# The third block's second group of columns by 20 products instead of 22, and an earlier place for the weight sums

## The chip, the cores and the metric

The kernel runs on one core of a Trainium2 chip. The time is that of one execution on the device in microseconds (us); less is better. Three runs of the kernel before gave a median of 463.58 us. The core has TensorE (matmuls, into the eight banks of PSUM), VectorE and ScalarE (both read PSUM and write on-chip memory), GpSimd, and SyncE, whose queue issues the transfers. In the profile they are PE (PEld for the loading of weights), DVE, ACT, POOL and SP.

## What is computed

A gated recurrence over a sequence, for 4 x 8 heads of 48 channels and 768 steps, is followed by a feed-forward part on 3072 tokens. All is fp32.

```python
for t in range(S):
    state = f[:, :, t, :, None] * state + np.einsum('bhd,bhe->bhde', k[:, :, t], v[:, :, t])
    y[:, :, t] = np.einsum('bhd,bhde->bhe', q[:, :, t], state)
x = np.ascontiguousarray(y.transpose(0, 2, 1, 3)).reshape(B * S, H * D)   # 3072 x 384
a = x @ w1            # 384 x 1024
b = x @ w2            # 384 x 1024
h = a * b @ w3        # 1024 x 1024
return h @ w_out      # 1024 x 384
```

`w3 @ w_out` is folded into one matrix of 1024 x 384 in the kernel, so each token block goes up (`a`, `b`, their product) and down (one matrix).

## The kernel before

The sequence is cut into 24 chunks of 128 steps (u = 0 to 23), and the tokens into six blocks of 512 (n = 0 to 5), each of four chunks. A chunk passes through `front` (loads, gates, forward and backward scans on VectorE, factors Q and K, L526 to L556), a visit of TensorE (L579, L653, L672, L686), state sums on VectorE (L759, L762, L818) and a way through DRAM that turns its result into columns of the block's xt (L866, L869). The 24th chunk is over at about 256 us; from then on there is only feed-forward work.

The up part of a block has three forms:

- `part` (block 0): plain products.
- `seven(jc)` (blocks 1 and 2, four calls each): a Strassen-like scheme for two column tiles and two token halves, over three tiles of the inner dimension. It has the parts m1, m2, m6, m5, m7, m4 and m3, which hold 1, 2, 1, 1, 2, 2 and 2, so 11 products; each product is made for w1 and for w2, two matmuls of 128x128 by 128x256 (L993). ScalarE copies partial results (L1034, L1037), and VectorE adds (L1043) and multiplies a by b (L1040, L1046). Its token sums (`sums`) and weight sums (`w12t`, made early) lie in the tile `place`.
- `many(g)` (blocks 3 to 5, two calls each): a scheme of 20 products for four column tiles, two token halves and three inner tiles, where two `seven` take 22. Its products (L1148) stand in six chains (`CHAINS`); a chain owns a bank, and after a product that is used by itself ScalarE copies the bank (L1169) before the next product of the chain is added to it. In CHAINS, (a, b) is token operand a with weight operand b. Operands a from 6 are the 12 token sums X (`X_SUMS`, L1115, one set for a block); operands b from 12 are the 22 weight sums (`W_SUMS`, L1109, one set for the kernel). VectorE adds the products up by the 12 `Y_SUMS` (L1192) and multiplies a by b (L1204, and L1211 after a half copy L1208).

The down part is two calls of `down` in a block, each with seven products of four matmuls of 128x192 (L897, which `part` uses too), sums of its operands S0 to S3 (L1262) and of its results (L1275, L1288, L1299, L1305, L1313), two copies (L1269, L1282), and stores (L1318).

The weight sums have no buffers of their own. They are written over tiles of the attention (`homes`): floor, the two gates, the three q, two k, two f, then fwd, bwd, K, K and Q. The temporaries of `many` lie in a pool "t" of nine: the first four are those of `seven` (`aside` frees them when the last `seven` are done), the others lie in Q and ys tiles. Block 2's token sums X lie where `w12t` does.

Before the end the kernel checks the range of its inputs: ScalarE looks at all weights again in 34 pieces (L1536, L1540), which SP loads (L1532) into three buffers; VectorE joins the counts (L1548 to L1569), the verdict goes to DRAM and back as one row (L1574, L1578), and L1583 and L1584 reduce it. A branch on it closes the program.

The order of instructions is made by a planner when the program is built (`Plan`): each piece of work is added with an engine, a cost, dependencies, a priority (the lowest goes first among those that can start), and what it takes and frees in slots and pools (banks are the pool "f"). `listed` then plays the engines in time and emits the pieces in that order, so a change of one piece's cost or priority can move all that follow, on every queue. [...]

The weight sums have the priority `100 * MANY + W_LATE + k`, and depend on `over`: the last chunk's visit, sums and transfers. `SPREAD` is what the planner allows for a transfer of the verdict to land.

Of the kernel before, what the change touches and what calls it, by code (L numbers as in the profile page):

```python
# [66 lines left out]
KH = KF // 2  # L67
# [23 lines left out]
GAP = 0.2  # L91
FILL_FROM = 262.0
RELOAD = 6.0
SPREAD = 10.0
QLATE = 0.1
MANY = 3
W_LATE = 30
W_SINCE = 0.0
W_STEP = 0.0
CHAINS = [  # L100
# [193 lines left out]
def ranged(ctx, tc, q, k, f_logit, v, w1, w2, w3, w_out, out, ident, w12, wc, left):  # L294
# [71 lines left out]
    plan = Plan()  # L366
# [85 lines left out]
    tk = [{} for _ in range(NU)]  # L452
# [268 lines left out]
    def turning(u):  # L721

        s, t = st[u], tk[u]

        def turned():
            s["kt"] = work.tile([P, HP, R], F32, name="kt")
            nc.scalar.copy(s["kt"].rearrange("p (b two) r -> p b (two r)", two=2), s["pk"])

        if u < NPE:
            t["t"] = plan.add("PE", 0.45, lambda: turn(u), [t["k"]] + past(u, 1, "d"), need(u) - 999)  # L730
        else:
            t["t"] = plan.add("PE", 0.45, lambda: turn(u), [t["k"]], need(u) - 999, takes=["f"])
        t["e"] = plan.add(
            "ACT", 0.55, turned, [t["t"]] + past(u, 2, "s"), need(u), frees=[t["t"]] if u >= NPE else [],
        )

    def begin(u):

        def emit():
            pairs(u)  # L740
            update(u)

        t = tk[u]
        t["a"] = t["s"] = plan.add(
            "PE", 1.1, emit, [t["q"], t["k"], t["e"], t["lv"]] + past(u, 1, "m", "d"), need(u) - 999, slack=0.8,
        )
        paired(u)
# [142 lines left out]
    blk = [{} for _ in range(NB)]  # L890
    stores, upq, downq, w_nodes, opened = [], [], [], [], []
    over = plan.add("none", 0.0, lambda: None)

    def three(out_, lhs, rhs, start=True):

        for i in range(len(lhs)):
            nc.tensor.matmul(  # L897
                out_, lhsT=lhs[i], rhs=rhs[i], start=start and i == 0, stop=i == len(lhs) - 1,
                skip_group_check=True,
            )  # L900

    def ffn(n):
# [16 lines left out]
        def part(c0, c1, jcs):  # L919
            cols = slice(c0 * C, c1 * C)  # L920
            nt = (c1 - c0) * C
            cost = 6 * max(0.135, nt * 0.322 / 384)

            def up(jc, which):
                def emit():
                    s["pu", jc, which, c0] = bank()
                    three(
                        s["pu", jc, which, c0][:, 0:nt], [up_weights(w12, which, kc, jc) for kc in range(KM)],
                        [s["xt"][:, kc, cols] for kc in range(KM)],
                    )  # L930
                return emit

            def keep_a(jc):
                return lambda: nc.scalar.copy(a_b(jc)[:, cols], s["pu", jc, 0, c0][:, 0:nt])

            def times(jc):
                def emit():
                    ab = a_b(jc)[:, cols]
                    nc.vector.tensor_tensor(ab, s["pu", jc, 1, c0][:, 0:nt], ab, ALU.mult)
                return emit  # L940

            for jc in jcs:
                h = jc // KH
                x = [tk[n * UB + c]["x"] for c in range(c0, c1)]
                n0 = 100 * n + 50 + 10 * (jc >= KH)
                pa = plan.add("PE", cost, up(jc, 0), x + pieces[0, h], n0, takes=["f"])
                ka = takes_ab(jc, plan.add("ACT", 0.2 + nt * 0.28 / 384, keep_a(jc), [pa], -10, frees=[pa]))
                pb = plan.add("PE", cost, up(jc, 1), x + pieces[1, h] + [pa], n0 - 5, takes=["f"])
                kb = plan.add("DVE", 0.16 + nt * 0.4 / 384, times(jc), [pb, ka], -10, frees=[pb])
                s["up"] += [pa, pb]  # L950
                s["done"][place_of(jc) // KH].append(kb)
# [134 lines left out]
        def x_node(i):  # L1086

            return quarter(i % KM, i // KM) if i < 2 * KM else at(n % 2 * 3072 + X_SUMS[i - 2 * KM][3] * TH, TH)

        def x_task(i):  # L1090
            return [s["X", i - 2 * KM]] if i >= 2 * KM else [tk[n * UB + c]["x"] for c in range(UB)]

        def w_view(i):

            if i < KM * 4:
                return w12[:, :, i % 4 // 2, i // 4].rearrange("p w (g b c) -> p w g b c", g=2, b=2)[:, :, :, i % 2]
            return home(W_SUMS[i - 4 * KM][3]).rearrange("p (w g c) -> p w g c", w=2, g=2)
# [5 lines left out]
        def op(o):  # L1103
            return ALU.add if o == "+" else ALU.subtract

        def many_sums():
            for k, (i, o, j, h) in enumerate(W_SUMS if not w_nodes else []):
                def emit(i=i, o=o, j=j, k=k):
                    nc.vector.tensor_tensor(w_view(4 * KM + k), w_view(i), w_view(j), op(o))  # L1109
                w_nodes.append(plan.add("DVE", 0.69, emit, [over] + w_nodes[-1:], 100 * MANY + W_LATE + k, since=W_SINCE + W_STEP * k))  # L1110
            old = [q[nm] for m in (n - 1, n - 2) for q in blk[m].get("seven", []) for nm in ("m5", "m6", "m7", "m4", "m3")]
            old += blk[n - 2].get("many", [])
            for k, (i, o, j, h) in enumerate(X_SUMS):
                def emit(i=i, o=o, j=j, k=k):
                    nc.vector.tensor_tensor(x_node(2 * KM + k), x_node(i), x_node(j), op(o))  # L1115
                before = [s["X", k - 1]] if k else old
                s["X", k] = plan.add("DVE", 0.43, emit, before + x_task(i) + x_task(j), 100 * n + 30 + k)
                s["up"].append(s["X", k])

        def many(g):  # L1120

            if ("X", 0) not in s:
                many_sums()
# [92 lines left out]
        if n >= MANY:  # L1216
            for g in range(2):
                many(g)
        elif n == 0:
            part(0, 2, range(KH))  # L1220
            part(2, 4, range(KH))
            part(0, 2, range(KH, KF))
            part(2, 4, range(KH, KF))
        else:
            for jc in range(KH):
                seven(jc)
            if n == MANY - 1:
                for q in s["seven"][-2:]:
                    for nm in ("e11", "e22", "e21", "e12"):
                        q[nm]["frees"].append(aside)  # L1230
# [129 lines left out]
        for i in range(UB // 2):  # L1360
            q = down(i)
# [74 lines left out]
    def weights():  # L1436
        due = dict(zip(((0, 0), (1, 0), (0, 1), (1, 1)), DUE))
        for item in (x for x in EARLY if x in "ABCD"):
            half, which = divmod("ABCD".index(item), 2)
            w = (w1, w2)[which]  # L1440
            cols = slice(half * KH * P, (half + 1) * KH * P)
            pieces[which, half] = fetch(
                [(kc * KH * P, KH * P, w[kc * P : kc * P + P, cols].unsqueeze(1)) for kc in range(KM)],
                EARLY_AT[item], turn_of(item), due[which, half],
                lambda which=which, half=half: w12[:, which, half].rearrange("p k c -> p (k c)"),
            )
# [140 lines left out]
    for u in range(NU):  # L1587
        if u <= SOLO:
            front(u)
        if NPE <= u <= SOLO:  # L1590
            turning(u)
            begin(u)
        if u >= SOLO and u + 1 < NU:
            front(u + 1)
            turning(u + 1)
        rest(u)
        if u == 0:
            weights()
        if u == 3:
            folding()  # L1600
        if u == NU - 1:
            late = plan.add("none", 0.0, lambda: None)
            plan.pools["f"] += [late] * 4
            for nm in ("y", "mid", "m", "v"):
                tk[u][nm]["frees"].append(late)
            over["deps"] += [tk[u][nm] for nm in ("z", "v", "mid", "k", "q", "y")] + [tk[u - 1]["z"]]
            weighed = [ranges()] if wide else []
            looked = plan.add("DVE", 1.0, judge, [tk[i]["y"] for i in range(NU)] + weighed, -20)
            sent = moves(1, 0.4, 250, told, [looked], 0, SPREAD)
            judged = plan.add("DVE", 0.2, decided, [moves(1, 0.4, 250, heard, [sent], 0, SPREAD)], -20)  # L1610
        if u % UB == UB - 1:
            ffn(u // UB)
# [13 lines left out]
    for t in plan.order():  # L1626
        if t["eng"] == "PE" and t["at"] < FULL:
            n = int((t["at"] - ready_at) / 0.43)
# [382 lines left out]
```

## Time and profile before

| | us |
|---|---|
| median of three runs | 463.58 |
| lowest and highest | 462.87, 463.83 |
| the profiled execution | 464.25 |
| its span in the trace | 462.5 |

The trace covers 462.5 of the 464.25 us; the other 1.75 us lie around it. The granted clock of TensorE is full throughout. The 40 slices show where each engine works (tenths of busy time, 11.6 us a slice):

```profile
PE   7999999999999999999999999999999999999995
DVE  8988899999898999988973599885658566768441
ACT  4565343432233553443323356566675666672000
POOL 9330000211223432223222000000000000000000
```

TensorE is full from the second slice on. VectorE is as full up to about slice 20, which is the attention, and again in slices 24 and 25, where the 22 weight sums are; after that it has gaps. Costly groups of the part that is changed (count | busy us, mean ns of one | idle time before):

```profile
L993 PE MATMUL f<-xt,w 128*128 128x256 f32 x140 | 36.2, 380 | 0.0
L993 PE MATMUL f<-place 128*128 128x256 f32 x84 | 22.4, 385 | 0.0
L1540 ACT ACTIVATE A<-A,back 128x512 f32<-128x512 f32 x23 | 17.9, 778 | 0.2
L1262 DVE TENSOR_TENSOR place<-ab 128x512 f32<-128x512 f32 x24 | 16.5, 689 | 1.0 <-PE f L897 0.9
```

An fp32 matmul leaves two records in the trace, so a product of `seven` or `many` counts four.

### The profile page before, as it was taken

To read this page: it belongs to the slowest core of one execution; us is meant where nothing else is said; L and a number is where in the kernel's file an instruction comes from. 1 tells how busy PE (TensorE), PEld (TensorE's weight loads), DVE (VectorE), ACT (ScalarE), POOL (GpSimd) and SP (SyncE) were. 2 spreads that over 40 slices of the span, in tenths; PEclk is the share of its full clock that TensorE was granted. 3 is DMA by queue.
4 is the path that set the end of the run, shared out by engine and by line. 5 is a ranking of instruction groups with operands and counts; after the bars stand their busy time and mean duration, and the time that the engine had idled before them with its cause. 6 is when DMAs were issued, how large, how long until landed. Compare 5 with 4: busy or idle time off the path is not lost.

```text
span 462.5 us, 11749 instructions
## 1 busy us (share of the span) xinstructions
PE 452.9 (98%) x4800; PEld 395.5 (86%) x4800; DVE 362.1 (78%) x633; ACT 208.6 (45%) x468; POOL 63.9 (14%) x90
## 2 busy tenths in 40 slices
PE   7999999999999999999999999999999999999995
PEld 6788885666899888888998888998898988889995
DVE  8988899999898999988973599885658566768441
ACT  4565343432233553443323356566675666672000
POOL 9330000211223432223222000000000000000000
PEclk9999999999999999999999999999999999999999
DMA  6896997833246764447324337653265523200111
GB/s 181 272 331 206 336 353 254 267 104 103 70 125 178 213 185 125 111 124 191 102 55 114 112 94 216 201 157 125 95 184 170 192 69 96 89 1 0 35 69 39
DMA packets 43309, 68.75 MB, mean 149 GB/s; under 512 B 5217, under 2 KB 28386, under 8 KB 42226
## 3 DMA queue, kind: packets, MB, share of 16 engines
q1 hardware_dynamic: 43250, 67.95, 47.8%
q8 instruction: 39, 0.64, 0.6%
q14 instruction: 20, 0.16, 0.1%
HBM read 58.88 MB, written 9.04 MB: 147 GB/s over the span
## 4 chain that ended last, share of the span: by engine, by line
PE 94%; POOL 2%; DVE 2%; issue 0%; POOLq 0%; DVEq 0%
PE f L897 25%; PE f L993 15%; PE f L1148 11%; PE f L1464 9%; PE py L1148 6%; PE pa L1148 5%; PE py L897 4%; PE pa L897 4%; PE py L653 3%; PE pa L579 2%; PE pa L686 2%; PE f L593 2%; PE py L672 2%; PE py L993 1%; POOL ab L437 1%; PE f L399 1%
## 5 line engine op out<-in xcount | busy, mean ns | idle before, releaser
L709 POOL TENSOR_SCALAR_AFFINE_SELECT A<-A 64x512 f32<-64x512 f32 (+1 forms) x46 | 42.3, 920 | 110.6 <-ACT A L703 108.5
L1464 PE MATMUL f<-place 128*128 128x384 f32 x128 | 42.4, 487 | 0.0
L897 PE MATMUL f<-xt,w 128*128 128x256 f32 x192 | 42.1, 380 | 0.0
L897 PEld LDWEIGHTS f<-xt,w 128*128 128x128 f32 x192 | 36.3, 190 | 5.0
L1464 PEld LDWEIGHTS f<-place 128*128 128x128 f32 x128 | 23.9, 190 | 15.5
L993 PE MATMUL f<-xt,w 128*128 128x256 f32 x140 | 36.2, 380 | 0.0
L897 PE MATMUL f<-place 128*128 128x192 f32 x192 | 34.8, 327 | 0.0
L897 PEld LDWEIGHTS f<-place 128*128 128x128 f32 x192 | 31.5, 190 | 0.3 <-issue 0.2
L548 DVE TENSOR_TENSOR_SCAN bwd<-gate,back 112x512 f32<-112x512 f32 x24 | 30.4, 1268 | 0.7
L526 DVE TENSOR_TENSOR_SCAN fwd<-gate,floor 112x512 f32<-112x512 f32 x24 | 30.0, 1251 | 1.2 <-ACT gate L518 0.3
L993 PEld LDWEIGHTS f<-xt,w 128*128 128x128 f32 x140 | 26.3, 190 | 3.5
L845 ACT ACTIVATE ys<-py 112x512 f32<-112x512 f32 x22 | 13.1, 596 | 32.7 <-PE py L672 28.1
L1400 ACT ACTIVATE place<-place 128x512 f32<-128x512 uint32 (+2 forms) x24 | 21.3, 888 | 9.1 <-DMA place<-in_w_dram 7.9
L897 PE MATMUL f<-wc,ab 128*128 128x192 f32 x128 | 23.6, 328 | 0.0
L993 PE MATMUL f<-place 128*128 128x256 f32 x84 | 22.4, 385 | 0.0
L897 PEld LDWEIGHTS f<-wc,ab 128*128 128x128 f32 x128 | 21.3, 190 | 0.4
L518 ACT ACTIVATE gate<-f 112x512 f32<-112x512 f32 x22 | 13.9, 632 | 17.0 <-DMA f<-in_f_logit_dram 7.9
L809 POOL TENSOR_TENSOR G<-lasts,gate 112x4 f32<-112x4 f32 x20 | 11.0, 549 | 76.4 <-ACT lasts L531 30.4
L653 PEld LDWEIGHTS py<-A,vt 64*64 64x64 f32 (+1 forms) x672 | 13.3, 127 | 7.3 <-issue 6.5
L653 PE MATMUL py<-A,vt 64*64 64x64 f32 (+1 forms) x672 | 18.1, 223 | 0.2
L1540 ACT ACTIVATE A<-A,back 128x512 f32<-128x512 f32 x23 | 17.9, 778 | 0.2
L1262 DVE TENSOR_TENSOR place<-ab 128x512 f32<-128x512 f32 x24 | 16.5, 689 | 1.0 <-PE f L897 0.9
(355 smaller groups left out, 1045.6 us busy)
## 6 DMA issues: line engine op xcount, KB each, us to landing
place<-in_w_dram SPq DMA_DIRECT2D x21, 512.0 KB, 6.1
A<-in_w_dram SPq DMA_DIRECT2D x19, 512.0 KB, 4.1
place<-in_w_dram SPq DMA_DIRECT2D x8, 1024.0 KB, 5.9
q<-in_q_dram SPq DMA_DIRECT2D x46, 96.0 KB, 2.6
vt<-in_v_dram SPq DMA_DIRECT2D x23, 192.0 KB, 3.1
out_dram<-o SPq DMA_DIRECT2D x23, 192.0 KB, 2.1
k<-in_k_dram SPq DMA_DIRECT2D x44, 96.0 KB, 2.4
yt<-ys SPq DMA_DIRECT2D x44, 96.0 KB, 2.9
```

What stands on the lines that cost most here:

```text
L518: nc.scalar.activation(gate[u % 2][:, 0:NQ], fu, AF.Sigmoid)
L526: nc.vector.tensor_tensor_scan(s["P"], gate[u % 2][:, 0:NQ], floor, 0.0, ALU.mult, ALU.max)
L548: nc.vector.tensor_tensor_scan(s["R"][:, ::-1], gate[u % 2][:, NQ:0:-1], back[:, ::-1], 0.0, ALU.mult, ALU.max)
L653: done = nc.tensor.matmul(y_block(u, hp, par, half)[p0 : p0 + w], lhsT=s["v"][half * W : half * W + W, h * D : h * D + w], rhs=s["A"][half ...
L709: nc.gpsimd.affine_select(out=a, in_=a, pattern=pattern, compare_op=ALU.is_ge, fill=0.0, base=0, channel_multiplier=-1,)
L897: nc.tensor.matmul(out_, lhsT=lhs[i], rhs=rhs[i], start=start and i == 0, stop=i == len(lhs) - 1, skip_group_check=True,)
L993: nc.tensor.matmul(q[nm][:, which * TH : which * TH + TH], lhsT=lhs[i](which), rhs=rhs[i], start=start and which == 0 and i == 0, stop=i = ...
L1148: nc.tensor.matmul(banks[g, c][:, which * TH : which * TH + TH], lhsT=lhs, rhs=x_node(a), start=first and which == 0, stop=True, skip_grou ...
L1262: nc.vector.tensor_tensor(abs_[j], x, y, op)
L1400: nc.scalar.activation(part_.bitcast(F32), part_, AF.Copy, bias=2.0, scale=2.0**-51)
L1464: nc.tensor.matmul(w3s["p", jc], lhsT=w3s[jc][:, kc * P : kc * P + P], rhs=wos[:, kc], start=(kc == 0), stop=(kc == KF - 1),)
L1540: return lambda: nc.scalar.activation(a, a, AF.Sign, bias=small, accum_out=counts[:, i : i + 1])
```

## The change

Block 2 (the third) still calls `seven` for its first two pairs of columns, 0 and 1. For the other half of the columns it calls `many(1)`. With it come its own token sums X and the weight sums, which are now wanted one block earlier. The weight sums whose place is one of the first twelve homes wait for `fronts` (the last chunk's backward scan and its factors K and Q, and the last gain G) and no longer for `over`; the others still wait for `over`. They remain in one chain, so each waits for the one before. Their priority becomes 336 + 0.1 k, where block 3's token sums have 330 and above. The token sums also wait for the same block's `seven`. `SPREAD` goes from 10 to 8.

```diff
-SPREAD = 10.0
+SPREAD = 8.0
 QLATE = 0.1
 MANY = 3
-W_LATE = 30
+
+NFRONT = 12
+W_SOON = 336.0
...
     over = plan.add("none", 0.0, lambda: None)
+    fronts = plan.add("none", 0.0, lambda: None)
...
-                w_nodes.append(plan.add("DVE", 0.69, emit, [over] + w_nodes[-1:], 100 * MANY + W_LATE + k, since=W_SINCE + W_STEP * k))
-            old = [q[nm] for m in (n - 1, n - 2) for q in blk[m].get("seven", []) for nm in ("m5", "m6", "m7", "m4", "m3")]
+                w_nodes.append(plan.add("DVE", 0.69, emit, [over if h >= NFRONT else fronts] + w_nodes[-1:], W_SOON + 0.1 * k, since=W_SINCE + W_STEP * k))
+            old = [q[nm] for m in (n, n - 1, n - 2) for q in blk[m].get("seven", []) for nm in ("m5", "m6", "m7", "m4", "m3")]
...
-            for jc in range(KH):
+            mixed = n == MANY - 1
+            for jc in range(KH // 2 if mixed else KH):
                 seven(jc)
-            if n == MANY - 1:
+            if mixed:
+                many(1)
                 for q in s["seven"][-2:]:
                     for nm in ("e11", "e22", "e21", "e12"):
                         q[nm]["frees"].append(aside)
...
+            fronts["deps"] += [tk[u][nm] for nm in ("r", "k", "q")] + [tk[u - 1]["G"]]
             over["deps"] += [tk[u][nm] for nm in ("z", "v", "mid", "k", "q", "y")] + [tk[u - 1]["z"]]
```

Line numbers in the texts are those of the kernel before.

## The prediction

> **What bounds the kernel now.** I read the page first (shares, then the chain that ended last), then TensorE's waits and busy time by stretch, then VectorE's order around the places the change touches.
>
> ```profile
> PE 452.9 (98%) x4800; PEld 395.5 (86%) x4800; DVE 362.1 (78%) x633; ACT 208.6 (45%) x468; POOL 63.9 (14%) x90
> PE 94%; POOL 2%; DVE 2%; issue 0%; POOLq 0%; DVEq 0%
> ```
>
> TensorE carries 94% of the chain. By stretch (sum columns: PE, PEld, DVE, ACT, POOL busy):
>
> ```profile
> 255.00:285.00 30.00, 30.00 (x177) 26.25 (x165) 24.04 (x42) 14.73 (x36) 0.00 (x0) 1.00 0.39 121
> 285.00:300.00 15.00, 15.00 (x85) 14.30 (x85) 12.10 (x28) 9.01 (x22) 0.00 (x0) 1.00 0.76 236
> 350.00:360.00 10.00, 9.43 (x51) 8.51 (x50) 8.75 (x19) 5.99 (x14) 0.00 (x0) 1.00 0.35 121
> ```
>
> From 255 us to the last matmul (end at about 457.3) TensorE is full except once. The waits of TensorE between 350 and 400 hold that hole, and the chain shows what made it, three sums of `many` in a row:
>
> ```profile
> PE py L897 <- DVE ys L1192: 0.6, 1, 0.6
> ...
> 353.15 0.70 DVE a L1192
> 353.86 0.02 issue
> 353.88 0.70 DVE ys L1192
> 354.58 0.02 issue
> 354.60 0.70 DVE ys L1192
> ```
>
> So after 255 us a matmul less is time less, one for one, and a VectorE or ScalarE instruction costs nothing until TensorE meets its result too early. One product in the same chain is two matmuls of 128x256, 0.86 us (four records); four steps of the chain show it, and that products follow each other with no gap:
>
> ```profile
> 314.59 0.86 PE py L1148 x4
> 315.46 0.86 PE pa L1148 x4
> 316.32 0.86 PE f L1148 x4
> 317.18 0.86 PE py L1148 x4
> ```
>
> The distance of the starts is 0.864 us; that is my price.
>
> [...] L759 waits 2.41 us for a copy while nothing passes it.
>
> **The change, part by part** (the order of instructions in the built programs is the same up to about 241 us).
>
> *TensorE.* Removed: `seven` for columns 2 and 3 of block 2, 2 x 11 products. Added: `many(1)`, 20 products. 2 x 0.864 = **1.73 us less**, all of it in the full stretch. Downs, fold and attention keep their counts.
>
> *ScalarE.* 12 copies L1169 come for 6 of L1034, one half copy L1208 for two of L1037: about 6 x 0.585 - 0.37 = 3.1 us more. From 255 to 300 it is busy 23.7 of 45 us: hidden.
>
> *VectorE.* Out: 14 instructions (6 of 0.69, 8 of 0.42 us, 7.5 us). In: 12 sums X (0.42), 12 sums Y (0.69), 8 products (0.42): 16.7 us. Net 9.2 us more, besides the 22 weight sums (0.69 each) that move. Four places decide whether that is seen.
>
> (a) Weight sums in the attention. Five now stand before the state sums of chunk 22:
>
> ```profile
> 240.85 0.36 DVE L1305 TENSOR_TENSOR o<-f,place 128x192 f32<-128x192 f32 x1
> 243.62 0.36 DVE L759 TENSOR_TENSOR A<-pa,S 112x192 f32<-112x192 f32 x1 [2.41 <-ACT A L703]
> ```
>
> Their starts lie 0.61 us apart, or 0.72 where one reads the one before (as at 279.90, 280.50, 281.22). From 241.1 that ends at 244.35, L1299 follows at 244.68 with its matmul, L759 at 244.96: 1.3 us late. TensorE reads its result at 248.8 and overwrites its bank at 247.9, so it waits for nothing. The next four, q2 apart, put chunk 23's L759 at 250.9 instead of 250.47, read at 255.1. The rest run where VectorE idled 2.07 and 4.06 us. Their cover is that idle time; without it, five sums cost 3.3 us. I take 0; by the distances above this could at most be 0.5.
>
> (b) Between the second `seven` and `many(1)`. TensorE stands at 257.2 as before. Its new order: two products on raw operands (to 258.9), m4 and m3 (to 262.4), four more on raw X (to 265.8), then (8,28), which needs X8. VectorE cannot write X before m3, as they lie on the factors' place: c12 at 262.6, e12 at 263.3, X6 to X8 to about 264.8. One microsecond to spare; X11 at 266.0 is needed at 268.4, X16 at 269.5 at 271.9. Cost 0.
>
> (c) Block 3's X8 follows block 2's Y sums and is ready at about 279.0, needed at 280.5. The weight sum bwd for (10,31) is ready at 289.5, needed at 290.9.
>
> (d) Block 2's first down, m6, needs its sum S1. From c12 (262.6) to S1 VectorE has 34 instructions of 512 and 41 of 256 columns. At 0.66 and 0.39 us from start to start (means over 279.9 to 286.9, and over the X sums at 289.0 to 291.4) this is 22.4 + 16.0 = 38.4 us; waits for copies that my walk meets add 3.4: S1 is there at 304.4. TensorE has, from 257.2, 49 products (42.3 us), m4 and m3 (3.45) and two pieces of a down of 1.30 us before m6: at 305.6. So **1.2 us of slack** at a stretch where VectorE is packed to 92%.
>
> *SP.* Block 4's four loads of xt wait for block 2's last product, now at 297.8 instead of 283.2; they took 4.2 to 5.2 us, so all are in at about 305, and first used at 305.6. They stand ahead of three loads of the range check, whose data ScalarE asks for at about 309: hidden, with 4 us left.
>
> *The verdict.* SPREAD 8 and the new plan move its sums behind the fourth `down` sum of block 4's second half:
>
> ```profile
> 417.26 0.18 DVE L1548 TENSOR_SCALAR back<-back 128x34 f32<-128x34 f32 x1
> 442.03 0.26 DVE L1583 TENSOR_REDUCE least<-row 1x1 f32<-1x128 f32 x1
> 419.10 0.33 SPq L1574 DMA_DIRECT2D good<-good  x1
> 430.79 0.32 SPq L1578 DMA_DIRECT2D row<-good  x1
> ```
>
> They now begin near 430.5 and are sent at 432.3. Out takes 7.0 us (median to landing): 439.3. Back took at most 442.03 - 430.79 = 11.2: 450.5. VectorE asks at 451.7, ahead of the sum that the last m3 needs. Free, but from both sides: nothing, or about 1 us if both ways run 1 us long. I take 0.
>
> *The sum.* -1.73, and the hole of 0.57 us at 355, which the old order of banks made. My walk over the second half finds no other, but it found slacks of 0.6 to 1.3 us, and one of them may fail. I keep a hole of that size: from 464.25 (span 462.5) to 462.5. The median before is 463.58, 0.67 below the profiled execution: **461.8**.
>
> **Rivals.** For all of them about 0.2%, 0.93 us, is what a measurement of this kernel can tell from no change.
>
> *Saved and given back* (chance 0.19). The products are gone, but two slacks of 0.6 to 1.3 us fail by about a microsecond: 462.7 to 464.5, say 463.5. For it: VectorE gains 9.2 us where it was busy 24.04 of 30. Against it: in the old kernel a stretch of the same build, from 300 to 350, shows no wait of TensorE.
>
> *VectorE becomes the bound from 262 to 306* (0.15, the slower side). Place: the packed order of (b) to (d). In it a copy on ScalarE that stands behind a range look (0.78 + 0.19 = 0.97 us) holds the whole VectorE queue. At four hops (t11, t16, block 3's t11, the last half copy) that is 3.9 us. Less the slack of 1.2 this is 2.7 us of standing TensorE, more than the 1.73 saved; if (b) and (c) stand too, 3.5: 465.3. It decides from 2.9 us of lateness at S1. Against it: my walk already has the looks in it and meets only two.
>
> *The verdict comes last* (0.03, within the two above in time): 3 us late at L1583 gives 463.6 or so.
>
> *Clean and the hole gone too* belongs to the forecast: 461.2.
>
> That the change doesn't do what it says is out: the built order has the 20 products, 40 matmuls, in place of 44.
>
> **How the numbers follow.** Forecast 0.63, its own range 461.1 to 462.4; given back 0.19; VectorE 0.15; verdict 0.03. Faster by over 0.2% means under 462.65: the forecast and a part of the next, 0.66. Within: 0.19. Slower: 0.15. Range: below 461.0 only if other holes close that I don't see (0.04); above 464.4 lies the slower rival (0.15). So 461.0 to 464.4.
>
> **What would show it.** TensorE busy about 451.2 us; no wait of TensorE over 0.5 us between 255 and 310; X8 of block 2 before 265.8; L759 of chunk 22 about 1.3 us later with TensorE unmoved; block 2's first m6 begun with its weights waiting for nothing; L1583 without idle time before it. Wrong: TensorE waits for L1109, L1115, L1192 or L1262 in that stretch, or L1583 released by its DMA.

## The result

The changed kernel takes **470.82 us** (median of 6 runs, 470.35 to 472.54) where the kernel before takes 463.49 (6 runs, 462.58 to 463.83): 1.0165 times the time, 95% interval 1.0147 to 1.0184. (Times here are medians, ratios are of the means.) It is 7.3 us slower. The forecast was 461.8, its range ended at 464.4; the forecast, the range and the sign of the change were wrong.

The changed kernel's page, its busy times and the shares of its chain (line numbers above L896 are three to five higher than before: product L1151, copy L1172, sum L1195, pieces of a down L900):

```profile
PE 456.3 (97%) x4792; PEld 394.0 (84%) x4792; DVE 370.6 (79%) x651; ACT 211.4 (45%) x473; POOL 68.5 (15%) x90
PE 92%; DVE 3%; ACT 2%; issue 1%; DMA 1%; SPq 0%; DVEq 0%; ACTq 0%
```

The eight matmul records less of the change are there (4792 for 4800), and so are VectorE's 8.5 and ScalarE's 2.8 us more. But the weight loads' share went from 86% to 84%, and VectorE and ScalarE stand in the chain with 5% where they had 2%: TensorE now waits. Its waits from 255 us to the end (who waited <- for whom: us in total, times, longest):

```profile
PE py L900 <- DVE place L1293: 0.9, 2, 0.5
PE py L900 <- DVE o L1304: 0.9, 2, 0.5
PE py L1151 <- DVE ab L1214: 0.9, 1, 0.9
PE py L1151 <- ACT a L1172: 0.6, 2, 0.3
PE pa L1151 <- DVE place L1195: 0.6, 1, 0.6
PE py L1151 <- ACT ys L1172: 0.3, 1, 0.3
PE py L1151 <- ACT place L1172: 0.3, 1, 0.3
PE pa L1151 <- ACT Q L1172: 0.3, 1, 0.3
PE pa L1151 <- ACT a L1172: 0.3, 1, 0.3
PE pa L1151 <- ACT ys L1172: 0.3, 1, 0.3
PE pa L900 <- DVE a L1195: 0.3, 1, 0.3
```

The reader is to see two things. The waits are many and small, spread from 271 to 454 us, most of them in blocks that the change does not touch. And the name on the left is always `pa` or `py`, never `f`, though `f` holds half of the banks.

I counted the loss from TensorE's starts: the distance of two starts less 0.864 us for a product and 1.30 for a piece of a down. From 255 us on these gaps come to 1.03 us in the kernel before and 10.32 in the changed one. 10.32 - 1.03, less the 1.73 us of the two products, is 7.56; TensorE's last matmul ends at 464.80 in place of 457.26, 7.54 later. So the saving was made, and holes took it back five times over.

What a hole looks like is seen in two views of the changed kernel, TensorE's and ScalarE's timelines at 268 us (start, duration, engine, line, operation, out<-in; the last bracket is idle time and who ended it):

```profile
268.51 1.03 PE L1151 MATMUL py<-place,gate 128*128 128x256 f32 x4
269.37 1.03 PE L1151 MATMUL py<-place,w 128*128 128x256 f32 x4
270.24 1.03 PE L1151 MATMUL pa<-place,q 128*128 128x256 f32 x4
271.61 1.99 PE L1151 MATMUL py<-place,f 128*128 128x256 f32 x8 [0.34 <-ACT a L1172]
```

```profile
270.48 0.58 ACT L1172 COPY ys<-py 128x512 f32<-128x512 f32 x1 [1.14 <-PE py L1151]
270.96 0.59 ACT L1172 COPY a<-py 128x512 f32<-128x512 f32 x1
```

The first two products belong to two chains. They write two banks; both are called `py`, because the four places that the attention leaves are handed out as halves of two tiles, `pa` and `py`, of two banks each. The first product ends at 269.54, and its copy to ys could start then. It starts at 270.48, just after the product into the other bank has ended at 270.40. The second copy follows at once; in the built program it has no wait on TensorE of its own, since the copy ahead of it has waited for both. Then the third product into py, which goes on in the first one's bank, starts 0.06 us after the second copy, out of the other bank, has ended at 271.55. The built program asks for both: the first copy waits for a count of TensorE's that is raised only with the second product, and the third product for the count that the second copy raises.

### The profile page after: what moved, and what is told of

It reads as the page before. It is cut to its first block, busy times and chain, and to the rows that moved or that the text cites. A ratio compares the mean times of both kernels' runs of the same rounds, so it can differ in the third digit from the quotient of the medians.

```text
span 469.0 us, 11776 instructions
## 1 busy us (share of the span) xinstructions
PE 456.3 (97%) x4792; PEld 394.0 (84%) x4792; DVE 370.6 (79%) x651; ACT 211.4 (45%) x473; POOL 68.5 (15%) x90
## 4 chain that ended last, share of the span: by engine, by line
PE 92%; DVE 3%; ACT 2%; issue 1%; DMA 1%; SPq 0%; DVEq 0%; ACTq 0%
PE f L900 24%; PE f L996 12%; PE f L1151 10%; PE f L1469 9%; PE py L1151 8%; PE pa L1151 7%; PE pa L900 5%; PE py L900 4%; PE py L655 3%; PE pa L581 2%; PE pa L688 2%; PE f L595 2%; PE py L674 2%; PE f L401 1%; DVE fwd L528 1%
## 5 line engine op out<-in xcount | busy, mean ns | idle before, releaser
L711 POOL TENSOR_SCALAR_AFFINE_SELECT A<-A 64x512 f32<-64x512 f32 (+1 forms) x46 | 45.5, 989 | 108.0 <-ACT A L705 105.9
L900 PE MATMUL f<-xt,w 128*128 128x256 f32 x192 | 42.1, 380 | 0.0
L900 PEld LDWEIGHTS f<-xt,w 128*128 128x128 f32 x192 | 36.3, 190 | 5.0
L1469 PEld LDWEIGHTS f<-place 128*128 128x128 f32 x128 | 23.9, 190 | 15.5
L900 PE MATMUL f<-place 128*128 128x192 f32 x176 | 31.9, 327 | 0.0
L996 PE MATMUL f<-xt,w 128*128 128x256 f32 x120 | 31.3, 380 | 0.0
L900 PEld LDWEIGHTS f<-place 128*128 128x128 f32 x176 | 28.9, 190 | 0.4 <-issue 0.2
L996 PEld LDWEIGHTS f<-xt,w 128*128 128x128 f32 x120 | 22.5, 190 | 2.9
L900 PE MATMUL f<-wc,ab 128*128 128x192 f32 x128 | 23.6, 328 | 0.0
L811 POOL TENSOR_TENSOR G<-lasts,gate 112x4 f32<-112x4 f32 x20 | 12.3, 613 | 75.0 <-ACT lasts L533 29.3
L900 PEld LDWEIGHTS f<-wc,ab 128*128 128x128 f32 x128 | 21.2, 190 | 0.3
L996 PE MATMUL f<-place 128*128 128x256 f32 x72 | 19.1, 386 | 0.0
L558 DVE TENSOR_TENSOR K<-k,bwd 112x512 f32<-112x512 f32 x22 | 16.9, 770 | 0.4
```

Of the source, the lines that this page charges most:

```text
L558: nc.vector.tensor_tensor(s["K"], ku, s["R"], ALU.mult)
L711: nc.gpsimd.affine_select(out=a, in_=a, pattern=pattern, compare_op=ALU.is_ge, fill=0.0, base=0, channel_multiplier=-1,)
L900: nc.tensor.matmul(out_, lhsT=lhs[i], rhs=rhs[i], start=start and i == 0, stop=i == len(lhs) - 1, skip_group_check=True,)
L996: nc.tensor.matmul(q[nm][:, which * TH : which * TH + TH], lhsT=lhs[i](which), rhs=rhs[i], start=start and which == 0 and i == 0, stop=i = ...
L1469: nc.tensor.matmul(w3s["p", jc], lhsT=w3s[jc][:, kc * P : kc * P + P], rhs=wos[:, kc], start=(kc == 0), stop=(kc == KF - 1),)
```

## The experiments

**Theory 1**: waits are kept for a tile, not for a bank. A read of one half of `pa` or `py` waits for a later product into the other half, and a product into one half waits for the read of the other. **Theory 2**: VectorE's extra 9.2 us make results late. **Theory 3**: the planner's new order leaves too little slack anywhere. In the built program reads of the two tiles can be counted that stand behind a later product into the other half: 16 of 92 before, 31 of 108 after.

### Tiles of one bank

```diff
-    ps = ctx.enter_context(tc.tile_pool(name="ps", bufs=1, space=PSUM))
     ps_f = ctx.enter_context(tc.tile_pool(name="ps_f", bufs=1, space=PSUM))
+    pairs_of = ctx.enter_context(ExitStack())
+    ps = pairs_of.enter_context(tc.tile_pool(name="ps", bufs=1, space=PSUM))
...
-            if nm not in found:
-                found[nm] = ps.tile([P, 2, NQ], F32, name=nm)
-            return found[nm][:, plan.got % 2]
+            if "ps2" not in found:
+                pairs_of.close()
+                found["ps2"] = ctx.enter_context(tc.tile_pool(name="ps2", bufs=1, space=PSUM))
+            return found["ps2"].tile([P, TB], F32, name=f"{nm}{plan.got % 2}")
```

In the changed kernel:

> The changed kernel with its order untouched; only the two last PSUM tiles of two banks each (pa, py), once the attention is done with them, become four tiles of one bank. Theory 1 (a reader of one half of pa or py is made to wait for a product into the other half, and the reverse): the holes of TensorE before pa and py, 10.0 of the 10.3 us of gaps after 255 us, go; TensorE's last matmul ends near 455 instead of 464.8, and the time is about 461 us, 460.7 to 462.5. Theory 2 (VectorE's 9.2 us more and its early sums of weights make results late): nothing changes but which product meets the lateness, 469.5 to 471. Theory 3 (the planner's new order leaves too little slack between any product and the copy it needs): the same, about 470.

Measured: **460.59 us** (22 runs), 0.9944 of the kernel before (0.9933 to 0.9955). In the built programs each engine's list of instructions is the same as in the changed kernel; only banks are named anew. The trace answers the question for TensorE's waits from 255 us on with no row, and its last matmul ends at 455.26. The same products and copies as above, with the tiles cut:

```profile
269.20 1.03 PE L1153 MATMUL py<-place,gate 128*128 128x256 f32 x4
270.06 1.03 PE L1153 MATMUL py<-place,w 128*128 128x256 f32 x4
270.93 1.03 PE L1153 MATMUL pa<-place,q 128*128 128x256 f32 x4
271.79 1.89 PE L1153 MATMUL py<-place,f 128*128 128x256 f32 x8
```

```profile
270.26 0.59 ACT L1174 COPY ys<-py 128x512 f32<-128x512 f32 x1 [0.28 <-PE py L1153]
271.13 0.59 ACT L1174 COPY a<-py 128x512 f32<-128x512 f32 x1 [0.28 <-PE py L1153]
271.99 0.59 ACT L1174 COPY a<-pa 128x512 f32<-128x512 f32 x1 [0.28 <-PE pa L1153]
```

The first copy now starts 0.03 us after its own product's end (270.23), while the next product is writing the neighbouring bank. Copies keep step with products, one in 0.86 us, and TensorE meets each in time. So this copy and this product ran side by side in two banks without loss (from this product's start to the next it is 0.87 us); the wait was in the program. Waits by single banks were enough in this run, and a guard of two banks costs 470.82 - 460.59 = 10.2 us here.

In the kernel before, the same edit:

> The same edit in the kernel before. Theory 1: its one hole, 0.74 us before a py product at 355 us, goes, and nothing else: 462.7 us, ratio about 0.998. Theories 2 and 3: 463.5, ratio 1.000.

Measured: 462.32 us (22 runs), ratio 0.9979 (0.9970 to 0.9988). The one hole that the prediction had found, at 355 us, is gone with it: it was of the same kind. Between the two kernels with cut tiles lie 462.32 - 460.59 = **1.73 us**, the two products. That it fits to the hundredth is luck: by the means it is 1.6, and each ratio is known to about 0.5 us.

### The same order, other pairs

```diff
-            nm = ("pa", "py")[(plan.got - NF) // 2]
+            nm = ("pa", "py")[plan.got % 2]
...
-            return found[nm][:, plan.got % 2]
+            return found[nm][:, (plan.got - NF) // 2]
```

This is done in the kernel before, so the change is not in it.

> The kernel before with its order untouched; only which two of the four late places share a tile is changed (first with third, second with fourth, in place of first with second, third with fourth). In the built program 26 reads then stand behind a later product into the other half of their tile, where the kernel before has 16 and the changed kernel 31. Theory 1: holes like those of the changed kernel appear in a kernel without the change; in proportion to the reads, (26-16)/(31-16) of 7.3 us: 468 us, 465 to 470. Theories 2 and 3: 463.5, as no instruction of TensorE, VectorE or ScalarE moves.

Measured: 467.45 us (5 runs), ratio 1.0089 (1.0066 to 1.0111). The unchanged kernel loses 4 us by the names of its banks alone. Its waits of TensorE in the same stretch have the same form:

```profile
PE py L1148 <- ACT ys L1169: 1.0, 2, 0.7
PE pa L897 <- DVE place L1288: 0.9, 2, 0.5
PE pa L897 <- DVE o L1299: 0.5, 1, 0.5
PE py L1148 <- ACT Q L1169: 0.3, 1, 0.3
```

Theories 2 and 3 cannot give this, since no engine's list of instructions changed but for the banks.

### One tile cut, the other kept

Of the changed kernel's holes of over 0.2 us, 2.56 us stand before `pa` and 5.87 before `py`. The edit is that of the cut tiles, with one tile excepted ("pa" here, "py" in the second run):

```diff
+            if nm == "pa":
+                if nm not in found:
+                    found[nm] = found["ps2"].tile([P, 2, NQ], F32, name=nm)
+                return found[nm][:, plan.got % 2]
             return found["ps2"].tile([P, TB], F32, name=f"{nm}{plan.got % 2}")
```

`py` alone is cut:

> The changed kernel with py alone cut into two tiles of one bank; pa stays one tile of two. The changed kernel's holes before pa are 2.56 us of 8.43, which is 3.1 of the 10.2 us that cutting both won: Theory 1: 463.7 us, 462.2 to 465. Rival (one of the two is the whole of it, and the other's holes only move): 460.6 or 468 and more.

Measured: 463.81 us (14 runs), ratio to before 1.0002 (0.9987 to 1.0017). And `pa` alone:

> The changed kernel with pa alone cut; py stays one tile of two banks. The holes before py are 5.87 us of 8.43, 7.1 of the 10.2 us. Theory 1: 467.7 us, 466 to 469.2. Rival: 460.6 or 471.

Measured: 467.82 us (7 runs), ratio 1.0074 (1.0049 to 1.0100). What is left over 460.59 is 3.2 and 7.2 us, together 10.4, where cutting both won 10.2: the holes add up, and none merely moves to the other tile.

### Which part of the change does it

```diff
-            mixed = n == MANY - 1
+            mixed = False
...
-            if mixed:
-                many(1)
+            if n == MANY - 1:
```

> Only the other two parts of the change are kept: the sums of weights begin at the last chunk's factors, and SPREAD is 8; block 2 keeps its four groups of `seven`. In the built program 16 reads stand behind a later product into the other half of their tile, as in the kernel before. Theory 1 (shared tiles alone make the loss): 463.4 us, 462.8 to 464.0. Theory 2 (the early sums on VectorE cost something themselves): 464.5 to 467.

Measured: 463.23 us (22 runs), ratio 0.9994 (0.9983 to 1.0005). The early sums and SPREAD cost nothing that can be measured. So the loss comes with `many(1)` in block 2: with it the planner gives other places out of the eight to the products of the blocks that follow, and 31 reads stand behind a product into the other half, not 16.

### Is VectorE short of time?

With the tiles cut, the last products of block 2's `many(1)` on VectorE are written twice:

```diff
-                        nc.vector.tensor_tensor(target(), where_[r][:, 0:TH], where_[r][:, TH:TB], ALU.mult)
+                        for _ in range(2 if n == MANY - 1 else 1):
+                            nc.vector.tensor_tensor(target(), where_[r][:, 0:TH], where_[r][:, TH:TB], ALU.mult)
```

> The changed kernel with both tiles cut, and the last product of each factor of block 2's many(1) on VectorE (128x256, 0.42 us, 0.34 to 0.36 from start to start) written twice, some seven times: 2.5 us more for VectorE before S1 of block 2's first down. The profile with the tiles cut has S1 ended at 305.0 and its m6 begun at 306.3, 1.3 us of slack. Theory (TensorE sets the end, VectorE is 1.3 us short of doing so there): about 1.2 us are seen, 461.8 us, 461.2 to 462.6. Rival (VectorE's load doesn't decide at all): 460.6. Rival (VectorE is already the bound in this stretch): 463.1 or more.

Measured: 460.67 us (7 runs, 460.27 to 461.46), ratio to before 0.9931 (0.9904 to 0.9958), with 0.9944 for the cut tiles alone: nothing of the 1.2 us is seen, and my expectation was wrong, on the side of the first rival. VectorE's timeline of the kernel with cut tiles, and then of this one, shows where the 2.5 us went:

```profile
294.19 0.69 DVE L1197 TENSOR_TENSOR place<-place,ys 128x512 f32<-128x512 f32 x1 [1.49 <-ACT ys L1174]
...
304.33 0.68 DVE L1269 TENSOR_TENSOR place<-place,ab 128x512 f32<-128x512 f32 x1
```

```profile
293.65 0.69 DVE L1197 TENSOR_TENSOR place<-place,ys 128x512 f32<-128x512 f32 x1 [0.90 <-ACT ys L1174]
...
304.19 0.68 DVE L1270 TENSOR_TENSOR place<-place,ab 128x512 f32<-128x512 f32 x1
```

The second row of each is S1. VectorE's idle time ahead of a copy shrinks (1.49 to 0.90 us here; waits of 0.2 to 0.3 elsewhere vanish) and takes in the added work. S1 lies 2.00 us ahead of its m6 (306.33) in the first and 1.60 (305.79) in the second, start to start. The slack at S1 was not the whole cover: what VectorE waits for copies on the way there is cover too.

### A planner that knows

First with two places more in place of four, one half of each tile:

```diff
-            nm = ("pa", "py")[(plan.got - NF) // 2]
+            nm = ("pa", "py")[plan.got % 2]
...
-            return found[nm][:, plan.got % 2]
+            return found[nm][:, (plan.got - NF) // 2]
...
-            plan.pools["f"] += [late] * 4
+            plan.pools["f"] += [late] * 2
```

> The changed kernel with only two places more after the attention in place of four: one half of pa and one of py, so that no two chains share a tile, and the planner orders with six banks. Theory 1: no hole from sharing is left; what six banks cost in place of eight is not known, so 461 to 466 us, and no wait of TensorE for a copy out of another bank. Theories 2 and 3: two banks less can only make it worse, 471 us or more.

Measured: 463.58 us (14 runs), ratio to before 1.0003 (0.9993 to 1.0013): 7.2 us better than the changed kernel with two banks less. TensorE's two waits left, 0.68 us before an `f` and 0.39 before a `pa` product, are of this order's own, since no two chains share a tile. Of its 3.0 us over the kernel with cut tiles, 2.2 lie in the gaps of TensorE's starts from 255 us on (0.0 there); the rest stays open.

Then with all four places and the tiles as they were, but a dislike of a place whose partner is in use:

```diff
+PAIR = 5.0
...
-            return [e for e in ends if e[0] is not None]
+            shared_ = []
+            for e, i in ends:
+                h = self.pools[name][i ^ 1] if name == "f" and i >= NF else None
+                late = after(t, enders[id(h)]) if h else 0.0
+                if e is not None:
+                    shared_.append((e + (PAIR if late is None or late > max(e, free.get("PE", 0.0)) else 0.0), i, e))
+            return shared_
...
-                    at = max(at, min(ends)[0])
+                    at = max(at, min(ends)[2])
```

> The changed kernel with its two shared tiles kept, and the planner taught to shun them: a place whose partner in the same tile is still in use counts as 5 us later when a bank is chosen. In the built program 12 reads stand behind a later product into the other half, in place of 31. Theory 1: what is left of the loss goes with the reads, 12/31 of 10.2 us over 460.6: 464.5 us, 462.5 to 466. Rival (the order of the changed kernel, not the number of such reads, is what matters): 468 or more.

Measured: **461.48 us** (5 runs), ratio 0.9961 (0.9948 to 0.9975), faster than the range expected. One hole is left, of 0.51 us at 271.12, and one gap of 0.23. So the count of shared reads is a sign and not a price: 12 of them are left, and one is met by TensorE too early.

With this edit and the cut tiles' edit together:

> The same order with both tiles cut into one-bank tiles. Theory 1: nothing of the loss is left, and the order of the planner that shuns pairs may cost a little by itself: 460.6 to 461.8. Rival: within 0.5 us of the kernel with the same order and shared tiles.

Measured: 460.56 us (6 runs), ratio 0.9941 (0.9927 to 0.9955): as fast as the changed kernel's own order with cut tiles. With one bank to a tile no difference of the two orders is seen; with shared tiles it was 470.82 against 461.48. Both versions with cut tiles and the change, and the planner that shuns pairs, beat both kernels.

## Why the prediction was wrong

- **The step that failed** is the last of the sum: the hole of 0.57 us at 355 us, "which the old order of banks made", of which "I keep a hole of that size". In its place stand fourteen waits, and TensorE's gaps come to 10.3 us. The walk that "finds no other" does not speak of a bank's other half. I had the right suspect and did not price it. I took the view's three sums on VectorE for its making and a bank for a bank. In truth it was one of a kind (cutting the tiles in the kernel before removes it, for 1.0 us), and another sharing-out of the places could make many more. The number of reads of `pa` and `py` that stand behind a product into the other half, which the built program tells before any run, was 31 for 16. It gives no price, but would have put a heavy case on the slower side.
- **-1.73 us for two products**: right. It is 1.73 between the two kernels with cut tiles, and the changed kernel's gaps add up only with it.
- **ScalarE, 3.1 us, and VectorE, 9.2 us more**: 2.8 and 8.5 us in the page, both hidden where the tiles are cut.
- **(a)** The state sum of chunk 22 starts at 244.92 (forecast 244.96), the next at 250.87, TensorE unmoved; without the products the early sums cost nothing that is seen.
- **(b)** (8,28) starts at 265.80 in the changed kernel, 0.87 us after the product ahead of it: no hole. Right.
- **(c)** Block 3's (8,28) starts at 281.78 with no wait. Right.
- **(d)** S1 ended at about 304.4 and m6 began at 305.6 in the forecast; with cut tiles they are 305.0 and 306.3, 1.3 us of slack for 1.2. The walk was good, its reading too narrow: it priced VectorE's queue and not the waits by which the products got their banks. In the changed kernel TensorE loses 2.9 us in five holes between 271 and 306, four before products into `py` (the longest 1.03 us at 301.58, behind a VectorE product that reads half of `py`) and one before a piece of a down in `pa`; with the tiles cut all five are gone.
- **SP** and **the verdict**: free, as said. From 255 us on no wait of TensorE is for a transfer, and ScalarE has one of 0.3 us. The verdict is sent at 440.1, asked back at 447.4, and used at 461.2 with no idle time before it.
- **The rivals.** "Saved and given back" had the balance right, but at about a microsecond where 9.3 were lost. "VectorE becomes the bound from 262 to 306" had the sign, and part of its place. Its mechanism was not there: with the tiles cut TensorE waits for nothing in that stretch, and 2.5 us more for VectorE are not seen.
- **The signs.** No wait of TensorE over 0.5 us was to lie between 255 and 310 us; there is one of 0.87 at 301.58. A wait for L1192 of the kernel before in that stretch was named a sign of being wrong; one of 0.27 us came, at 305.15 (another, 0.56 at 393.77, lies outside). It shows how little the name of the last releaser says: those sums read `pa`, and it was the tile that made TensorE wait for them.

## What to carry to other kernels

In this program a tile that spans two PSUM banks is one thing to the waits, whoever writes and reads its halves (470.82 us with two such tiles, 460.59 with both cut). When the banks of such a tile are lent out singly, give each a tile of its own, or teach the planner that they are not independent. When a wait's left side carries always the same few buffer names, ask what these buffers share before asking which engine is late; and when a change alters which places of a pool are handed out, count in the built program, ahead of the run, the reads that stand behind a product into the neighbour.

## What the runs showed that was not expected

Here a wait of TensorE cost more than its idle time. The wait of 0.30 us at 274.76 moves the start of its product by 0.46, and the product after it starts 0.97 us later, not 0.864: 0.57 us in all. Each of the fourteen holes costs 0.24 to 0.27 us over its idle time, whether that is 0.27 or 0.87 us, so 5.6 us of idle time stand for 9.4 of the 10.3 us of gaps. Of this surplus 0.16 us is a matter of counting: a matmul of 256 columns has a record of 0.38 us, and in a full stream the next one starts 0.22 us after its start, and idle time is counted only from the record's end. The other 0.10 us follows inside the product that waited; why, no run shows. So here many short waits cost more than one long wait of the same idle time. The same holds for the hole of the kernel before: 0.57 us of idle time, 0.84 in starts, 1.0 us (0.6 to 1.4, from the ratio's interval) when it is gone.
